# Attention and a gated feed-forward block on one core: score blocks dealt evenly to straight and swapped tiles, another order of the transposes, other weights in the planner

## The chip, the cores and the metric

The kernel runs on one core of a Trainium2 chip. Time is device microseconds of one execution. Before the change the median of three runs is 417.66 us (417.26 to 417.67). The engines are called TensorE (PE in the profile, PEld for its weight loads), VectorE (DVE), ScalarE (ACT), GpSimd (POOL) and SyncE (SP, which issues the DMAs).

## The reference

Causal attention for 4 batches and 12 heads (448 positions, 64 columns a head), then a feed-forward block whose hidden rows are gated by a convolution over three positions. All is float32.

```python
scores = (q @ k.transpose(0, 1, 3, 2)) / np.sqrt(64)
scores = np.where(np.triu(np.ones((S, S), bool), k=1), -1e9, scores)
attn = np.exp(scores - scores.max(-1, keepdims=True))
attn = attn / (attn.sum(-1, keepdims=True) + 1e-9)
x = (attn @ v).transpose(0, 2, 1, 3).reshape(B, S, 768)
h = np.maximum(x @ w_in, 0)                  # 768 -> 1024
c = sum(conv_w[i] * hp[:, i:i + S] for i in range(3))   # hp: h padded by one row
out = (h * (1 / (1 + np.exp(-c)))) @ w_out   # 1024 -> 768
```

## The kernel before

**Attention.** Two heads make a pair, and there are 24 pairs, six for each batch. The rows of the score matrix are cut into seven blocks `k` of 64 queries, and block `k` needs only the keys up to its own end: `KEYS[k] = 64 * (k + 1)`, so 64 to 448 columns. Head `j` lies in partitions `64 * j` on, and each product (L407) uses a quarter of TensorE's array: rows `half(j)` and columns `half(j)`, or the other half for blocks with odd `k`. The first are called straight tiles here, the second swapped tiles. A block takes two products, one for each head. Blocks share four PSUM banks, `SCORES = ((6, 0), (5, 1), (4, 2), (3,))`.

The softmax of a block is a masked minimum of the negated scores (VectorE, L433), an exponential with its sum (ScalarE, L439), an addition and a reciprocal for a group of blocks (VectorE or GpSimd at L455, VectorE at L458), and a scaling by the reciprocal, called normalisation here (VectorE at L470 or ScalarE at L474). Groups are `RANK[:4]` and `RANK[4:]`. Then TensorE transposes the normalised blocks in sixteen 128x128 pieces (L493), four to a PSUM bank. Two banks take turns, and each is copied out (L502, ScalarE or VectorE) before the PV products (L521) use it. `BANKS` says which blocks a bank holds; banks 0 to 3 are filled in this order. Swapped blocks have their heads the wrong way round, and the transpose puts them right.

**Feed-forward.** An operand is split into a rounded upper part and a rest, and three products stand for one: weights upper with activations upper and rest, weights rest with activations upper (L563 for `w_in`, L616 for `w_out`). There are 1152 such products of 448 columns. The 32 weight tiles come as words that need integer steps on VectorE first (L289 or L292, L299 to L315), then a rounding (`round_ways`, L249 to L253: ScalarE, VectorE or GpSimd) and a subtraction for the rest (L263: VectorE or GpSimd). A hidden row block passes through a relu (L574, ScalarE), three taps (L594 on ScalarE or L579 on VectorE, then L581 twice), a tanh (L584), a product (L587), a rounding and a subtraction.

**What sets the order.** Nothing is written out by hand. Each step is added to a `Plan` with its engine, its cost, what it needs and makes, and other ways to do it. `Plan.run` (L64) takes again and again the step that can start first, and among its ways the one whose start plus `cost * WEIGHT` is least (L116). A way marked as holding the port is started only when the port shared by VectorE and GpSimd is free in the plan (L107), and keeps it until its end (L129). The order so found is the program's order on every engine. Pairs of batches 2 and 3 are paced: their scores wait for a count of feed-forward products of the batch before (L410 to L418), and all seven blocks are one step; the others are in two steps of four and three blocks. The planner's numbers that matter are

```python
OWN = {"PE": 0, "DVE": 115, "ACT": 145, "POOL": 40, "SP": 0}
WEIGHT = {"DVE": 1.2, "ACT": 1.0, "POOL": 0.5}
```

## Time and profile before

| what | us |
|---|---|
| median of three runs | 417.66 |
| the profiled execution | 418.87 |
| its span, first to last instruction | 417.1 |
| TensorE busy | 393.9 (94% of the span) |
| VectorE busy | 277.6 (67%) |
| ScalarE busy | 233.5 (56%) |
| GpSimd busy | 115.8 (28%) |

The granted clock of TensorE is 0.98 of full speed over the span. A busy share over the whole span mixes stages: VectorE's 67% is an average of a stage in which it is nearly always busy and of one in which it is busy half the time. A matmul's end is modelled in the trace, so a stretch of TensorE is read from the start of one row to the start of the next. The profile's instructions are two for a float32 product (a record for each of its two passes) and one for a transpose.

### The profile page before, as it was taken

The page shows a single profiled execution, that of the slowest core. Times are in us where ns is not written, and L with a number is a line of the kernel's source. Part 1 is how long each engine was busy: PE and PEld are TensorE (multiplying, and loading weights), DVE is VectorE, ACT ScalarE, POOL GpSimd, SP SyncE. Part 2 cuts the span into 40 slices and gives each one's busy share as a digit, 9 for nine tenths or more (in the row PEclk, how much of TensorE's full clock was granted, in tenths as well). Part 3 has the DMA queues.
Part 4 walks back from the last instruction along what each step waited for, and adds up shares of the span by engine and source line. Part 5 has one row for each costly group of instructions (what it writes and reads, how often), then busy time and mean ns, then how long its engine had stood idle before and what let it go on. Part 6 is the DMA issues. An engine that isn't in the chain of part 4 may idle for free.

```text
span 417.1 us, 7344 instructions
## 1 busy us (share of the span) xinstructions
PE 393.9 (94%) x2604; PEld 305.5 (73%) x2604; DVE 277.6 (67%) x820; ACT 233.5 (56%) x645; POOL 115.8 (28%) x146
## 2 busy tenths in 40 slices
PE   6979977996999999999999999999999999999996
PEld 2646544775766678778778878778778889999895
DVE  3799999999899995548877505548877500477200
ACT  2887886868897755547655616447655611233111
POOL 1032553654565461011231100012231100145300
PEclk9798999998999999999999999999999999999999
DMA  8944502222444743121210222121200011000111
GB/s 282 396 157 152 176 2 77 83 79 68 145 111 138 247 127 107 39 83 46 70 50 22 91 71 67 64 77 46 69 27 3 22 46 44 24 1 0 45 45 44
DMA packets 15156, 35.88 MB, mean 86 GB/s; under 512 B 1808, under 2 KB 4880, under 8 KB 15120
## 3 DMA queue, kind: packets, MB, share of 16 engines
q1 hardware_dynamic: 15120, 35.42, 25.9%
q8 instruction: 20, 0.33, 0.3%
q14 instruction: 16, 0.13, 0.1%
HBM read 29.91 MB, written 5.51 MB: 85 GB/s over the span
## 4 chain that ended last, share of the span: by engine, by line
PE 67%; DVE 23%; ACT 7%; issue 2%; POOL 0%; ACTq 0%; POOLq 0%
PE bank L616 25%; PE bank L563 20%; PE bank L493 8%; PE bank L407 7%; PE bank L521 7%; DVE bank L433 5%; DVE p L470 3%; DVE u L581 2%; DVE wraw L315 2%; DVE u L309 2%; ACT p L439 2%; DVE u L299 2%; ACT pt L502 2%; ACT p L474 1%; DVE u L303 1%
## 5 line engine op out<-in xcount | busy, mean ns | idle before, releaser
L563 PE MATMUL bank<-parts,wih 128*128 128x448 f32 x384 | 116.3, 378 | 3.1 <-DVE parts L537 1.8
L616 PE MATMUL bank<-parts,woh 128*128 128x448 f32 x384 | 114.4, 373 | 0.0
L439 ACT ACTIVATE p<-bank,negm 128x128 f32<-128x128 f32 (+6 forms) x168 | 77.9, 477 | 29.0 <-DVE negm L433 28.1
L563 PEld LDWEIGHTS bank<-parts,wih 128*128 128x128 f32 x384 | 71.8, 191 | 12.2 <-issue 3.6
L433 DVE CUSTOM_DVE_ANT_0 bank<-bank,mask 128x448 f32<-128x448 f32 (+6 forms) x168 | 69.0, 441 | 14.7 <-PE bank L407 12.4
L616 PEld LDWEIGHTS bank<-parts,woh 128*128 128x128 f32 x384 | 71.3, 188 | 8.0 <-issue 2.5
L563 PE MATMUL bank<-parts,wil 128*128 128x448 f32 x192 | 72.8, 379 | 0.0
L493 PE MATMUL bank<-ident,p 128*128 128x128 f32 x384 | 61.3, 288 | 10.5 <-ACT p L474 4.9
L616 PE MATMUL bank<-parts,wol 128*128 128x448 f32 x192 | 71.0, 370 | 0.0
L253 POOL TENSOR_SCALAR parts<-u 128x448 fp32r<-128x448 f32 x27 | 17.2, 638 | 191.4 <-DVE u L587 191.4
L493 PEld LDWEIGHTS bank<-ident,p 128*128 128x128 f32 x384 | 45.8, 145 | 25.0 <-ACT pt L502 9.0
L502 ACT COPY pt<-bank 128x512 f32<-128x512 f32 x89 | 49.9, 585 | 15.8 <-PE bank L493 15.3
L581 DVE SCALAR_TENSOR_TENSOR u<-hr,cw,u 128x448 f32<-128x448 f32 x64 | 50.6, 794 | 6.5 <-ACT u L594 5.1
L407 PE MATMUL bank<-raw 64*64 64x320 f32 (+6 forms) x672 | 51.7, 399 | 3.4 <-ACT p L439 3.2
L521 PE MATMUL bank<-pt,vraw 128*64 128x448 f32 (+3 forms) x384 | 47.3, 387 | 1.4 <-ACT pt L502 1.4
L407 PEld LDWEIGHTS bank<-raw 64*64 64x64 f32 x672 | 27.0, 137 | 26.7 <-issue 11.1
L521 PEld LDWEIGHTS bank<-pt,vraw 128*64 128x64 f32 x384 | 21.5, 137 | 25.7 <-issue 14.8
L563 PEld LDWEIGHTS bank<-parts,wil 128*128 128x128 f32 x192 | 36.7, 191 | 3.8 <-issue 1.1
L263 POOL TENSOR_TENSOR parts<-u,parts 128x448 fp32r<-128x448 f32 x31 | 38.2, 1235 | 2.2
L537 DVE TENSOR_TENSOR parts<-bank,parts 128x448 fp32r<-128x448 f32 x24 | 14.8, 617 | 35.9 <-ACT parts L534 35.6
L616 PEld LDWEIGHTS bank<-parts,wol 128*128 128x128 f32 x192 | 36.1, 188 | 3.4 <-issue 0.8
L627 ACT ACTIVATE u<-bank 128x448 f32<-128x448 f32 x24 | 13.0, 543 | 43.6 <-PE bank L616 42.9
(46 smaller groups left out, 389.9 us busy)
## 6 DMA issues: line engine op xcount, KB each, us to landing
raw<-in_qk_dram SPq DMA_DIRECT2D x24, 448.0 KB, 3.8
vraw<-in_v_dram SPq DMA_DIRECT2D x24, 256.0 KB, 3.0
wraw<-in_w_in_dram SPq DMA_DIRECT2D x16, 384.0 KB, 4.8
wraw<-in_w_out_dram SPq DMA_DIRECT2D x16, 384.0 KB, 3.2
out_dram<-u SPq DMA_DIRECT2D x24, 224.0 KB, 1.9
wraw<-in_conv_w_dram SPq DMA_DIRECT2D x1, 24.0 KB, 6.4
```

The costliest lines, as they stand in the source:

```text
L253: lambda: nc.gpsimd.tensor_scalar(out=out(), in0=src(), scalar1=1.0, scalar2=1.0, op0=ALU.mult, op1=ALU.mult),
L263: engine.tensor_tensor(out=out(), in0=src(), in1=f32(hi()), op=ALU.subtract)
L407: nc.tensor.matmul(at(s)[half(j ^ (k % 2)), o : o + KEYS[k]], lhsT=t[:, 1, 64 * k : 64 * k + 64], rhs=t[:, 0, : KEYS[k]], start=True, stop ...
L433: nc.vector.tensor_tensor_reduce(out=t, in0=t, in1=mask[:, S - n :], scale=-0.125, scalar=3.0e38, op0=ALU.add, op1=ALU.min, accum_out=negm ...
L439: nc.scalar.activation(at(p)[:, :n], at(s)[:, o : o + n], AF.Exp, bias=negm[g % 2][:, c : c + 1], scale=-1.0, accum_out=ssum[g % 2][:, c : ...
L493: nc.tensor.matmul(to, lhsT=at(("p", g, k))[:, P * kc : P * kc + P], rhs=ident, is_transpose=True)
L502: copy(at(part)[:, cols], at(pt))
L521: nc.tensor.matmul(at(pv)[half(j), S - n : S], lhsT=at(vraw)[:, kc, j], rhs=at(("pt", g, y))[:, o : o + 2 * n].rearrange("p (s j q) -> p s ...
L537: nc.vector.tensor_tensor(out=at(x)[:, 1], in0=at(pv)[:, :S], in1=f32(at(x)[:, 0]), op=ALU.subtract)
L563: nc.tensor.matmul(at(ph)[:, :S], lhsT=block(w, NCC * f + cc), rhs=at(x)[:, part], start=q == 0, stop=q == len(prods) - 1)
L581: nc.vector.scalar_tensor_tensor(out=t, in0=src, scalar=w, in1=t, op0=ALU.mult, op1=ALU.add)
L616: nc.tensor.matmul(at(po)[:, :S], lhsT=block(w, NF * m + f), rhs=at(g)[:, part], start=q == 0, stop=q == len(prods) - 1)
```

## The change

There are five edits. Block `k` is on a swapped tile if it is in `SWAPPED = (5, 4, 1, 0)`, and no longer if `k` is odd; the banks of the scores become `((6,), (5, 1), (4, 0), (3, 2))`. The order of the blocks in the scores and in the softmax follows, with groups of three and four blocks in place of four and three. The transpose banks are filled in the order 1, 3, 0, 2: banks 1 and 3 hold nothing but blocks 4 to 6, and the copies' dependences are turned accordingly. In the planner the weight of VectorE goes from 1.2 to 1.5, so that for a step that either engine can do a way on ScalarE is taken more often; and a rounding on GpSimd holds the shared port. The planned cost of the score steps goes from 1850 to 1650 and from 930 to 830.

```diff
-    WEIGHT = {"DVE": 1.2, "ACT": 1.0, "POOL": 0.5}
+    WEIGHT = {"DVE": 1.5, "ACT": 1.0, "POOL": 0.5}
...
-    SCORES = ((6, 0), (5, 1), (4, 2), (3,))
-    RANK = (6, 0, 5, 1, 4, 2, 3)
+    SCORES = ((6,), (5, 1), (4, 0), (3, 2))
+    SWAPPED = (5, 4, 1, 0)
+    RANK = (6, 5, 1, 4, 3, 2, 0)
...
                     out=out(), in0=src(), scalar1=1.0, scalar2=1.0, op0=ALU.mult, op1=ALU.mult
                 ),
+                True,
...
-                        at(s)[half(j ^ (k % 2)), o : o + KEYS[k]], lhsT=t[:, 1, 64 * k : 64 * k + 64],
+                        at(s)[half(j ^ (k in SWAPPED)), o : o + KEYS[k]], lhsT=t[:, 1, 64 * k : 64 * k + 64],
...
-                "PE", 1850, lambda: scores((6, 5, 0, 1, 4, 3, 2)), makes=[("scores", g, 0), ("scores", g, 1)], drop=[raw],
+                "PE", 1650, lambda: scores((6, 5, 1, 3, 4, 2, 0)), makes=[("scores", g, 0), ("scores", g, 1)], drop=[raw],
...
-            for i, blocks in enumerate(((6, 5, 0, 1), (4, 3, 2))):
+            for i, blocks in enumerate(((6, 5, 1), (3, 4, 2, 0))):
...
-        groups = RANK[:4], RANK[4:]
+        groups = RANK[:3], RANK[3:]
...
-        for y, pieces in enumerate(BANKS):
+        TURNS = (1, 3, 0, 2)
+        for z, y in enumerate(TURNS):
+            pieces = BANKS[y]
...
-                        if k % 2:
+                        if k in SWAPPED:
...
-            before_it = ((("pv", g - 1), 1), ("PT", g, 0, 1), ("PT", g, 1, 1), ("PT", g, 2, 1))
             plan.add(
-                "PE", 440, transp, needs=[*names, before_it[y]], mode=3,
+                "PE", 440, transp, needs=[*names, ("PT", g, TURNS[z - 1], 1) if z else (("pv", g - 1), 1)], mode=3,
...
-                needs=[(pt, 1)] + ([("pt", g, y - 1, 0)] if y % 2 else []), makes=[part, ("pt", g, y, 0)],
-                take=[] if y % 2 else [("pt", part)], drop=[pt],
+                needs=[(pt, 1)] + ([("pt", g, y + 1, 0)] if y % 2 == 0 else []), makes=[part, ("pt", g, y, 0)],
+                take=[("pt", part)] if y % 2 else [], drop=[pt],
```

**The scores of the 20th pair on TensorE,** in batch 3, before and after. A row gives the line, the operation, the bank written, the tile read, and the columns of one product; `x2` are the two heads.

```order
L407 MATMUL bank_135<-raw_204 64x448 x2
L407 MATMUL bank_136<-raw_204 64x384 x2
L407 MATMUL bank_135<-raw_204 64x64 x2
L407 MATMUL bank_136<-raw_204 64x128 x2
L407 MATMUL bank_137<-raw_204 64x320 x2
L407 MATMUL bank_138<-raw_204 64x256 x2
L407 MATMUL bank_137<-raw_204 64x192 x2
```

After the change, at the same place:

```order
L409 MATMUL bank_135<-raw_204 64x448 x2
L409 MATMUL bank_137<-raw_204 64x384 x2
L409 MATMUL bank_137<-raw_204 64x128 x2
L409 MATMUL bank_136<-raw_204 64x256 x2
L409 MATMUL bank_138<-raw_204 64x320 x2
L409 MATMUL bank_136<-raw_204 64x192 x2
L409 MATMUL bank_138<-raw_204 64x64 x2
```

Before, the blocks of 448, 64, 320 and 192 columns are on straight tiles (banks 135 and 137) and those of 384, 128 and 256 on swapped ones. After, 448, 256 and 192 are straight (135 and 136) and 384, 128, 320 and 64 swapped (137 and 138).

**The transposes of the same pair on TensorE,** with the feed-forward products between them. Here the names `p_0_215`, `p_0_216` and `p_0_217` are blocks 4, 5 and 6, `p_1_208`, `p_1_210`, `p_1_212` and `p_1_214` blocks 0 to 3; banks 139 and 140 take the transposes; a swapped block is written as `128x2x64`.

```order
L493 MATMUL bank_140<-ident,p_1_208 128x128
L493 MATMUL bank_140<-ident,p_1_210 128x2x64
L493 MATMUL bank_140<-ident,p_1_212 128x128
L493 MATMUL bank_140<-ident,p_1_214 128x2x64
L493 MATMUL bank_139<-ident,p_0_215 128x128
L493 MATMUL bank_139<-ident,p_0_216 128x2x64
L493 MATMUL bank_139<-ident,p_0_217 128x128 x2
L563 MATMUL bank_141<-parts,wih_66 128x448 x2
L493 MATMUL bank_140<-ident,p_1_212 128x128
L493 MATMUL bank_140<-ident,p_1_214 128x2x64
L493 MATMUL bank_140<-ident,p_0_215 128x128
L493 MATMUL bank_140<-ident,p_0_216 128x2x64
```

After the change, from the first transpose of the pair on:

```order
L497 MATMUL bank_140<-ident,p_0_215 128x2x64
L497 MATMUL bank_140<-ident,p_0_216 128x2x64
L497 MATMUL bank_140<-ident,p_0_217 128x128 x2
L497 MATMUL bank_139<-ident,p_0_217 128x128
L497 MATMUL bank_139<-ident,p_0_215 128x2x64
L497 MATMUL bank_139<-ident,p_0_216 128x2x64
L497 MATMUL bank_139<-ident,p_0_217 128x128
L566 MATMUL bank_141<-parts,wil_82 128x448
L566 MATMUL bank_141<-parts,wih_66 128x448
L497 MATMUL bank_140<-ident,p_1_208 128x2x64
L497 MATMUL bank_140<-ident,p_1_210 128x2x64
L497 MATMUL bank_140<-ident,p_1_212 128x128
```

Before, eight transposes that need all of blocks 0 to 6 come first, then four and four. After, eight that need blocks 4 to 6 alone come first, and then the other eight in one piece.

**ScalarE's queue in the softmax of the fifth pair,** in batch 0. `L439` is an exponential, `L474` a normalisation, `L502` a copy of transposes, `L289` and `L249` steps of a weight, `L534` a copy of a PV result.

```order
L439 ACTIVATE p_0_215,ssum_131<-bank_136,negm_129 128x320
L534 CAST parts<-bank_140 128x448
L439 ACTIVATE p_0_211,ssum_131<-bank_136,negm_129 128x192
L439 ACTIVATE p_0_213,ssum_131<-bank_137,negm_129 128x256
L474 ACTIVATE p_0_207<-p_0_207,rcp_133 128x64
L289 ACTIVATE u_220<-wraw 128x384
L289 ACTIVATE u_221<-wraw 128x384
L474 ACTIVATE p_0_213<-p_0_213,rcp_133 128x256
L502 COPY pt_218<-bank_139 128x512
L502 COPY pt_218<-bank_140 128x512
L289 ACTIVATE u_222<-wraw 128x384
L502 COPY pt_219<-bank_139 128x512
```

After the change (lines are two or three higher):

```order
L441 ACTIVATE p_0_207,ssum_131<-bank_137,negm_129 128x64
L537 CAST parts<-bank_139 128x448
L476 ACTIVATE p_0_217<-p_0_217,rcp_133 128x448
L291 ACTIVATE u_222<-wraw 128x384
L476 ACTIVATE p_0_209<-p_0_209,rcp_133 128x128
L476 ACTIVATE p_0_215<-p_0_215,rcp_133 128x320
L476 ACTIVATE p_0_211<-p_0_211,rcp_133 128x192
L291 ACTIVATE u_220<-wraw 128x384
L505 COPY pt_218<-bank_140 128x512
L505 COPY pt_219<-bank_139 128x512
L291 ACTIVATE u_221<-wraw 128x384
L505 COPY pt_218<-bank_140 128x512
```

Four normalisations stand on ScalarE in place of two, larger ones among them, and the copies go to the two halves in turn.

Steps that changed engine, counted in the program up to the first softmax step of the 13th pair (the first of batch 2) on VectorE's and on ScalarE's queue:

| step | VectorE before | after | ScalarE before | after |
|---|---|---|---|---|
| normalisation of 448 columns | 6 | 4 | 6 | 8 |
| of 320 | 6 | 2 | 6 | 10 |
| of 256 | 7 | 1 | 5 | 11 |
| of 192 | 2 | 3 | 10 | 9 |
| of 64 | 4 | 6 | 8 | 6 |
| copy of a transpose bank | 7 | 4 | 41 | 44 |
| copy of a PV result | 0 | 2 | 12 | 10 |
| first tap of the convolution | 2 | 0 | 6 | 8 |
| sign bit cleared, or magnitude | 6 | 4 | 26 | 28 |
| rounding of a weight | 0 | 0 | 2 | 12 |
| rounding of a gate | 0 | 0 | 3 | 4 |
| subtraction for a rest | 5 | 0 | | |
| addition before a reciprocal | 4 | 9 | | |

On GpSimd, over the whole program, roundings of weights go from 30 to 20, their subtractions from 28 to 32, roundings of gates from 27 to 23, subtractions there from 31 to 32. On TensorE 226 of the 1152 feed-forward products stand before the PV products of the 12th pair, and 222 after the change; the scores of the 13th pair come after 241 products, and now after 270.

## Rows read from the trace of the kernel before

**Rows 1.** Busy time of each engine in four stretches of the span (the third lies inside the second). Columns: from and to in us, length, then for PE, PEld, DVE, ACT and POOL the busy us and in brackets the number of instructions, the granted clock of TensorE as a share of full speed, the mean busy share of the DMA engines, GB/s.
```profile
0.00:22.30 22.30, 17.63 (x131) 9.75 (x131) 12.94 (x62) 12.13 (x41) 2.70 (x13) 0.85 0.92 335
22.30:152.90 130.60, 115.87 (x814) 80.71 (x814) 126.56 (x360) 103.18 (x288) 67.13 (x83) 0.97 0.39 121
40.00:61.30 21.30, 18.79 (x160) 11.15 (x152) 21.11 (x70) 18.22 (x54) 11.34 (x14) 1.00 0.30 104
152.90:417.10 264.20, 260.43 (x1663) 215.01 (x1662) 138.06 (x400) 118.15 (x317) 46.00 (x50) 1.00 0.14 48
```

**Rows 2.** The page's chain of work that ended last, as shares of the span by engine, and a piece of the same chain between 40 and 97 us. Columns of the piece: start, us, engine and tile and line, instructions.
```profile
PE 67%; DVE 23%; ACT 7%; issue 2%; POOL 0%; ACTq 0%; POOLq 0%
...
85.16 1.51 DVE u L581
```

**Rows 3.** Timeline of TensorE. First a pair of the fourth batch: its score matmuls and what TensorE started next; then a pair of the second batch of which only blocks 6, 5, 0 and 1 are run in one go. Columns: start us, length us up to the modelled end of the last, engine, line, operation, tiles, shape of the first, count of records. The next row's start shows when the engine was free.
```profile
293.56 1.95 PE L407 MATMUL bank<-raw 64*64 64x448 f32 x28
295.44 0.47 PE L563 MATMUL bank<-parts,wih 128*128 128x448 f32 x1
...
86.35 1.09 PE L407 MATMUL bank<-raw 64*64 64x448 f32 x16
87.37 0.47 PE L563 MATMUL bank<-parts,wil 128*128 128x448 f32 x1
```

**Rows 4.** Timeline of TensorE around the transposes of one pair (from 285.93) and of the next (from 300.61), with the feed-forward products between them. Columns as in rows 3.
```profile
285.93 1.03 PE L493 MATMUL bank<-ident,p 128*128 128x128 f32 x8
286.71 0.64 PE L563 MATMUL bank<-parts,wih 128*128 128x448 f32 x2
287.20 0.66 PE L493 MATMUL bank<-ident,p 128*128 128x128 f32 x4
287.61 0.45 PE L563 MATMUL bank<-parts,wil 128*128 128x448 f32 x1
287.90 0.60 PE L493 MATMUL bank<-ident,p 128*128 128x128 f32 x4
288.25 0.45 PE L563 MATMUL bank<-parts,wih 128*128 128x448 f32 x1
...
300.61 1.39 PE L493 MATMUL bank<-ident,p 128*128 128x128 f32 x8
301.75 0.45 PE L563 MATMUL bank<-parts,wil 128*128 128x448 f32 x1
302.04 0.36 PE L563 MATMUL bank<-parts,wih 128*128 128x448 f32 x1
302.24 0.66 PE L493 MATMUL bank<-ident,p 128*128 128x128 f32 x4
```

**Rows 5.** Groups of VectorE instructions between 22.3 and 152.9 us, shapes kept apart. Columns: line, engine, operation, tiles, output shape and input shape, count, busy us and mean ns of one, idle time before them and what ended it.
```profile
L502 DVE COPY pt<-bank 128x512 f32<-128x512 f32 x6 | 4.1, 684 | 0.2 <-PE bank L493 0.2
...
L470 DVE TENSOR_SCALAR p<-p,rcp 128x320 f32<-128x320 f32 x5 | 2.6, 530 | 0.0
...
L470 DVE TENSOR_SCALAR p<-p,rcp 128x256 f32<-128x256 f32 x6 | 2.3, 389 | 0.0
...
L292 DVE TENSOR_SCALAR u<-wraw 128x384 uint32<-128x384 uint32 x5 | 2.1, 421 | 0.0
L470 DVE TENSOR_SCALAR p<-p,rcp 128x448 f32<-128x448 f32 x4 | 2.1, 515 | 0.0
L263 DVE TENSOR_TENSOR wil<-wraw,wih 128x384 fp32r<-128x384 f32 x3 | 2.0, 670 | 0.0
...
L470 DVE TENSOR_SCALAR p<-p,rcp 128x64 f32<-128x64 f32 x3 | 1.8, 594 | 0.0
...
L579 DVE TENSOR_SCALAR u<-hr,cw 128x448 f32<-128x448 f32 x2 | 1.2, 588 | 0.0
```

**Rows 6.** Groups of ScalarE instructions in the same stretch, columns as in rows 5.
```profile
L502 ACT COPY pt<-bank 128x512 f32<-128x512 f32 x38 | 21.6, 582 | 5.0 <-PE bank L493 4.8
...
L289 ACT ACTIVATE u<-wraw 128x384 f32<-128x384 f32 x25 | 13.9, 566 | 4.2 <-DVE wraw L315 3.7 <-DMA wraw<-in_w_out_dram 0.4
...
L534 ACT CAST parts<-bank 128x448 fp32r<-128x448 f32 x10 | 5.4, 544 | 1.5 <-PE bank L521 1.5
...
L474 ACT ACTIVATE p<-p,rcp 128x448 f32<-128x448 f32 x6 | 4.0, 666 | 3.8 <-DVE rcp L458 3.8
L594 ACT ACTIVATE u<-hr,cw 128x448 f32<-128x448 f32 x6 | 4.0, 663 | 0.2 <-POOL parts L263 0.2
...
L474 ACT ACTIVATE p<-p,rcp 128x320 f32<-128x320 f32 x5 | 2.8, 556 | 1.7 <-DVE rcp L458 1.7
...
L474 ACT ACTIVATE p<-p,rcp 128x256 f32<-128x256 f32 x5 | 2.5, 497 | 0.0
...
L249 ACT CAST wih<-wraw 128x384 fp32r<-128x384 f32 x1 | 0.5, 544 | 0.0
```

**Rows 7.** Two neighbouring VectorE instructions, the GpSimd instruction that ran beside the second, and the group of GpSimd's weight subtractions between 22.3 and 152.9 us. Columns of the first three as in rows 3, of the last as in rows 5.
```profile
67.06 0.35 DVE L303 TENSOR_SCALAR u<-u 128x384 uint32<-128x384 uint32 x1
67.33 0.69 DVE L299 TENSOR_SCALAR u<-u 128x384 f32<-128x384 f32 x1
...
67.25 0.55 POOL L253 TENSOR_SCALAR wih<-wraw 128x384 fp32r<-128x384 f32 x1 [1.47 <-DVE wraw L315]
...
L263 POOL TENSOR_TENSOR wil<-wraw,wih 128x384 fp32r<-128x384 f32 x13 | 13.8, 1064 | 1.1
```

More of the change, by code (lines that the diff above doesn't have):

```diff
@@ L419, in pair @@
         else:
-            for i, blocks in enumerate(((6, 5, 0, 1), (4, 3, 2))):
+            for i, blocks in enumerate(((6, 5, 1), (3, 4, 2, 0))):
                 plan.add(
-                    "PE", 930, lambda blocks=blocks: scores(blocks), makes=[("scores", g, i)], drop=[raw], mode=1,
+                    "PE", 830, lambda blocks=blocks: scores(blocks), makes=[("scores", g, i)], drop=[raw], mode=1,
                     needs=[raw, ("scores", g, 0) if i else ("norm", g - 2)], take=[("S", ("S", g, 2 * i + z)) for z in range(2)],
                 )
-        groups = RANK[:4], RANK[4:]
+        groups = RANK[:3], RANK[3:]
         for i, blocks in enumerate(groups):
@@ L450, in pair @@
         for i, blocks in enumerate(groups):
-            cols = slice(4 * i, 4 * i + len(blocks))
+            cols = slice(3 * i, 3 * i + len(blocks))
             def r_sum(engine, cols=cols):
```

## Prediction

> **What bounds the kernel now.** I read the busy time by stretch first. It splits the span of 417.1 us in three [rows 1]. From 22.3 to 152.9 us VectorE is busy 126.56 of 130.6 us (97%), ScalarE 103.18 (79%), TensorE 115.87 (89%). From 152.9 us on TensorE is busy 260.43 of 264.2 us and VectorE 138.06. So VectorE sets the pace until about 153 us, TensorE after that. The first 22.3 us are start-up, with DMA at a share of 0.92.
>
> The chain of waits says the same [rows 2]: between 40 and 97 us it runs through VectorE, the taps at 85.16 being one of its longer pieces, and over the whole span TensorE's matmuls hold 67%. What the change does is therefore priced twice: in VectorE and ScalarE time before 153 us, and in TensorE time behind it.
>
> **Part 1: the score products.** In the timeline of TensorE a pair's 28 score matmuls (14 products; each float32 product leaves two records) take from 293.56 to the next work at 295.44, so 1.88 us [rows 3]. Where only blocks 6, 5, 0 and 1 are run, 16 matmuls take from 86.35 to 87.37, 1.02 us [rows 3]. Products on straight tiles and on swapped tiles run side by side; the longer of the two streams decides. Before, straight tiles (blocks 6, 4, 2, 0) carry 448+320+192+64 = 1024 columns and swapped ones (5, 3, 1) 768; for blocks 6, 5, 0, 1 it is 512 against 512. So 512 more columns cost 1.88 - 1.02 = 0.86 us, 1.68 ns a column. That the streams overlap follows from the same rows: 1792 columns at 1.68 ns one after the other would take 3.0 us and not 1.88. After the change straight tiles (6, 3, 2) carry 896 and swapped ones (5, 4, 1, 0) 896: 128 columns less on the longer stream, 128 x 1.68 = 0.215 us for each pair. The 12 pairs of batches 2 and 3 stand behind 152.9 us, where TensorE is the bound: 12 x 0.215 = 2.6 us. For the first 12 pairs I count nothing, since there TensorE waits for VectorE. Bounds: 0, if the even deal keeps one stream waiting for the other in some other way, and 24 x 0.215 = 5.2 us.
>
> **Part 2: the order of the transposes.** A pair now has transposes in three places on TensorE: eight from 285.93 to 286.71 (0.78 us), four from 287.20 to 287.61, four from 287.90 to 288.25 [rows 4], 1.54 us together. After, it is two places of eight, 1.56 us. Each return from transposes to products makes the first product about 0.29 us long (287.61 to 287.90) instead of 0.2 (302.04 to 302.24) [rows 4]; one return less saves 0.09 us, 12 pairs 1.1 us. Against it, the second eight need both transpose banks copied out first, and ScalarE takes 0.582 us for a copy [rows 6]. One such wait is seen: the eight at 300.61 take until 301.75, 1.14 us instead of 0.78 [rows 4]. A wait of 0.36 us in every pair would cost 4.3 us. Between -1.1 and +4.3 I take +0.3, because of the pairs I read only this one waited. Early normalisation of blocks 4 to 6 lets the first eight start sooner, but nothing waits there after 153 us.
>
> **Part 3: steps moved between VectorE, ScalarE and GpSimd.** The counts are those in the section on the change, up to the 13th pair, the stretch that VectorE bounds. VectorE loses, by the means of that stretch [rows 5]: 6 normalisations of 256 columns x 0.389, 4 of 320 x 0.530, 2 of 448 x 0.515, 3 transpose copies x 0.684, 2 taps x 0.588, 2 bit-clears x 0.421, and 5 rest subtractions x 0.670 (the row of three of them stands for all): 2.33 + 2.12 + 1.03 + 2.05 + 1.18 + 0.84 + 3.35 = 12.9 us. It gains 2 normalisations of 64 columns x 0.594, 2 casts of a PV result (sized by the copy out of the same kind of bank, 0.684), and 6 small steps (one normalisation of 192 columns and five additions on 3 or 4) that I put at 0.2 each: 3.8 us. Records overlap: an instruction of 0.35 us at 67.06 is followed by the next at 67.33, 0.08 earlier than its end [rows 7]. There are 24 steps less and 10 more, so 14 x 0.08 = 1.1 us comes off: VectorE is relieved of 12.9 - 3.8 - 1.1 = 8.0 us.
>
> ScalarE gains [rows 6]: 6 x 0.497 + 4 x 0.556 + 2 x 0.666 (normalisations), 3 x 0.582 (copies), 11 x 0.544 (roundings of ten weights and a gate), 2 x 0.663 (taps), 2 x 0.566 (magnitudes): 2.98 + 2.22 + 1.33 + 1.75 + 5.98 + 1.33 + 1.13 = 16.7 us. It loses 3 short normalisations (put at 0.4 each) and 2 casts x 0.544, 2.3 us. It has 25 steps more, and with the overlap taken as on VectorE 25 x 0.08 = 2.0 us come off 14.4. So it gains 12.4 us and stands at 103.2 + 12.4 = 115.6 us.
>
> GpSimd does 10 weight roundings less and 4 weight subtractions more. They touch VectorE too: while a rounding ran on GpSimd from 67.25 for 0.55 us, a VectorE step started at 67.33 took 0.69 us instead of the 0.35 of its neighbour [rows 7]. So each rounding gone frees 0 to 0.34 us, 0 to 3.4 us in all; each subtraction that arrives blocks 0 to its own length, 1.064 us [rows 7], 0 to 4.3 us in all. I take half of either: 8.0 + 1.7 - 2.1 = 7.6 us of relief for VectorE. On GpSimd's lock the Trainium skill says more, on its page "SBUF — State Buffer", section "SBUF: two separate sides": VectorE and GpSimd share one pair of ports, and whichever starts first holds it for its whole instruction while the other fully blocks. The row at 67.33 agrees; how often the two meet no page can say, and by it alone the relief could lie anywhere from 3.7 to 11.4 us.
>
> What becomes late next is ScalarE. If VectorE stays the bound with its 4.0 us of idle time, the stretch takes 130.6 - 7.6 = 123.0 us and ScalarE would be busy 94% of it. The highest share that a stretch shows for ScalarE is 18.22 of 21.30 us, 86%, from 40 to 61.3 [rows 1]; at that share 115.6 us of work need 135.1 us, 4.5 more than before. Behind each step added to ScalarE's queue stand the exponentials and the copies of the transposes, for which TensorE waits. VectorE has shown that a queue here can run at 97% once it is the one waited for, and ScalarE's 86% was measured while it was not. So I stand nearer to the first: two thirds of 123.0 and a third of 135.1 is 127.0 us, 3.6 us saved. One thing goes against it: when the 12th pair's PV products are reached, the new order has put 222 products of the feed-forward part before them, the old one 226. The 4 left for later cost 4 x 0.2 = 0.8 us, since TensorE is the bound from there.
>
> **The sum.** 418.87 us of the profiled execution (1.8 us outside the span) - 3.6 + 0.8 - 2.6 + 0.3 = 413.8. The median of the runs is 417.66, 1.2 us under it, so 412.6 us. Behind 153 us VectorE and ScalarE have slack (138.06 and 118.15 busy of 264.2 [rows 1]), so what is moved between them there costs nothing; without this cover each tap moved to ScalarE would make the way to its gate 0.663 - 0.588 = 0.1 us longer.
>
> **Rivals.**
> 1. ScalarE becomes the bound and the stretch to 153 us grows. For it: 12.4 us more on a queue that was never over 86% busy. Against: part of its idle time is waiting for VectorE, which goes as VectorE is relieved. At 86% the stretch costs +4.5; with the rest of the sum (0.8 - 2.6 + 0.3 = -1.5) the whole is 417.66 + 4.5 - 1.5 = 420.7 us. It decides the sign where ScalarE stays below 115.6 / (130.6 + 1.5) = 87.5%.
> 2. The two engines only change places and nothing is gained before 153 us; only TensorE's saving is left: 417.66 - 1.5 = 416.2 us. That is ScalarE at 115.6 / 130.6 = 88.5%.
> 3. VectorE remains the only bound and all relief counts: 417.66 - 7.6 - 1.5 = 408.6 us; with all 10 roundings having been in its way and none of the 4 subtractions, 417.66 - 11.4 - 1.5 = 404.8 us. The rule of the Trainium skill quoted above is a reason one would expect this.
> 4. The even deal doesn't shorten the scores, because one stream is held up by the order in which products are issued: only part 3 acts, 417.66 - 3.6 + 0.8 + 0.3 = 415.2 us. Against it: two streams of uneven length already run side by side in 1.88 us.
>
> **Chances.** Forecast 0.42; rival 1 0.14; rival 2 0.17; rival 3 0.20; rival 4 0.07. No change can be told within 0.2% (0.8 us). All cases but rival 1 lie below 416.8, rival 2 only just; so 0.10 for same (half of rival 2 and a rest of rival 1), 0.13 for slower and 0.77 for faster. The range from 406 to 419.5 leaves out the far end of rival 3 and of rival 1. The forecast's own range is 410 to 415.
>
> **What would show it.** Part 1: a pair's 28 score matmuls take 1.66 to 1.68 us behind 160 us; still 1.88 means rival 4. Part 2: two places of eight transposes; over 0.8 us for the second eight in most pairs means the copies hold them. Part 3: the PV products of the 12th pair start at about 149.3 instead of 152.9 us; VectorE's busy time falls by some 8 us before that point and ScalarE's rises by 12; if ScalarE's share stays at 86% or less and the point moves later, rival 1 holds. From that point to the end 264.2 us should shrink by 1.5.

## The result, and the profile after

The changed kernel takes 403.94 us (median of four runs, 402.56 to 404.97), the kernel before 417.67 beside it: a ratio of 0.966 (95% interval 0.962 to 0.970). The forecast was 412.6 us, with a range down to 406: 13.7 us were gained where 5 were expected. The profiled execution has a span of 400.8 us (before 417.1). These two spans differ by 16.3 us, more than the medians do: the profiled execution before was one of the longer ones of its kernel (418.87), the one after the shortest of its four (402.56).

Busy time by stretch, the view of [rows 1], with the cut at the 12th pair's PV products (135.7 us now, 152.9 before):

```profile
0.00:22.30 22.30, 16.72 (x144) 9.57 (x144) 14.32 (x72) 14.24 (x45) 2.67 (x13) 1.00 0.93 346
22.30:135.70 113.40, 106.58 (x794) 75.98 (x794) 106.03 (x326) 107.63 (x305) 57.45 (x67) 1.00 0.39 125
135.70:400.80 265.10, 260.39 (x1667) 216.77 (x1666) 136.33 (x386) 130.71 (x337) 52.24 (x64) 1.00 0.16 53
```

The first stage is 17.2 us shorter, the rest 0.9 us longer. Up to the cut VectorE is busy 14.32 + 106.03 = 120.4 us, before 12.94 + 126.56 = 139.5; ScalarE 121.9 after 115.3. In the second stretch VectorE (106.03 of 113.4) and ScalarE (107.63, 95%) are now even. The granted clock, 0.97 there before, is 1.00.

The chain of waits of the changed kernel, against [rows 2]:

```profile
PE 62%; DVE 18%; ACT 15%; issue 3%; POOL 1%; DMA 1%; ACTq 0%; DVEq 0%; POOLq 0%
```

VectorE went from 23% to 18% of the span, ScalarE from 7% to 15%: the chain changes between them.

TensorE's timeline in the changed kernel: transposes of one pair and the scores of a later one, columns as in [rows 3] and [rows 4].

```profile
284.23 1.09 PE L497 MATMUL bank<-ident,p 128*128 128x128 f32 x8 [0.50 <-DVE p L472]
285.08 0.66 PE L566 MATMUL bank<-parts,wih 128*128 128x448 f32 x2
285.57 1.13 PE L497 MATMUL bank<-ident,p 128*128 128x128 f32 x8
286.46 0.45 PE L566 MATMUL bank<-parts,wil 128*128 128x448 f32 x1
...
291.76 1.75 PE L409 MATMUL bank<-raw 64*64 64x448 f32 x28
293.43 0.67 PE L566 MATMUL bank<-parts,wih 128*128 128x448 f32 x2
```

Scores take 1.67 us from start to start (293.43 - 291.76) where they took 1.88. The transposes stand in two places: 0.85 us, and 0.89 us with no wait named.

VectorE's four bit steps on the weights, from 22.3 us to the 12th pair's PV products; first the kernel before, then the changed one. Columns as in [rows 5].

```profile
L315 DVE SCALAR_TENSOR_TENSOR wraw<-wraw,u 128x384 uint32<-128x384 uint32 x30 | 18.0, 601 | 0.1
L309 DVE SCALAR_TENSOR_TENSOR u<-wraw,u 128x384 uint32<-128x384 uint32 x29 | 16.9, 583 | 0.1
L303 DVE TENSOR_SCALAR u<-u 128x384 uint32<-128x384 uint32 x30 | 14.4, 480 | 0.1
L299 DVE TENSOR_SCALAR u<-u 128x384 f32<-128x384 f32 x30 | 13.8, 465 | 0.1
```

```profile
L317 DVE SCALAR_TENSOR_TENSOR wraw<-wraw,u 128x384 uint32<-128x384 uint32 x28 | 17.5, 628 | 0.1
L311 DVE SCALAR_TENSOR_TENSOR u<-wraw,u 128x384 uint32<-128x384 uint32 x28 | 15.6, 560 | 0.1
L301 DVE TENSOR_SCALAR u<-u 128x384 f32<-128x384 f32 x27 | 11.4, 425 | 0.1
L305 DVE TENSOR_SCALAR u<-u 128x384 uint32<-128x384 uint32 x27 | 10.6, 396 | 0.0
```

The same work on the same shapes takes 63.1 / 119 = 530 ns a step before and 55.1 / 110 = 501 ns now. Undisturbed such steps take 0.55 and 0.35 us; the rest is time in which GpSimd holds VectorE up. Two or three weight tiles are also converted later than before.

ScalarE's groups in the changed kernel, from 22.3 to 135.7 us, against [rows 6]:

```profile
L505 ACT COPY pt<-bank 128x512 f32<-128x512 f32 x38 | 20.5, 591 | 0.8 <-PE bank L497 0.8
...
L476 ACT ACTIVATE p<-p,rcp 128x448 f32<-128x448 f32 x8 | 5.7, 709 | 0.0
...
L476 ACT ACTIVATE p<-p,rcp 128x320 f32<-128x320 f32 x9 | 5.1, 565 | 1.2 <-DVE rcp L460 1.2
...
L250 ACT CAST wih<-wraw 128x384 fp32r<-128x384 f32 x7 | 3.9, 564 | 0.5 <-DVE wraw L317 0.4
```

The idle time ahead of copies fell from 5.0 to 0.8 us, that ahead of normalisations of 448 columns from 3.8 to 0: ScalarE's idle time was waiting for others, and it went.

**Two measures used below, both to the 12th pair's PV products.** *Blocked*: what VectorE's instructions (from the first pair's PV products on) took beyond their shape's undisturbed length, taken as the 20th percentile over all traces, where that is over 60 ns. *Stall*: the time of the mark less the work that TensorE had issued by then, at 0.203 us a feed-forward product, 0.103 a transpose, 1.883 a pair's PV products, a pair's scores as measured, and 4.0 for the twelve products on zeros at the start. It holds waits and lost clock alike. Before: blocked 17.1 us, stall 40.0. After: 8.7 and 26.1.

**The sum.** At the cut, 17.2 us are the stall's 13.9, 12 x 0.202 = 2.4 of scores, and 0.8 for four products fewer before it. Behind it: scores -2.4, transposes +1.1, those four products +0.8, and the rest mostly new waits before the first transposes of a few pairs (0.50 us at 284.23 above, 0.62 at 191.34): +0.9. Together that is the 16.3 us between the two traces.

### The profile page after: what moved, and what is told of

Its sections match the earlier page's. It is cut to its first block, busy times and chain, and to the rows that moved or that the text cites. A ratio compares the mean times of both kernels' runs of the same rounds, so it can differ in the third digit from the quotient of the medians.

```text
span 400.8 us, 7332 instructions
## 1 busy us (share of the span) xinstructions
PE 383.7 (96%) x2604; PEld 302.3 (75%) x2604; DVE 256.7 (64%) x782; ACT 252.6 (63%) x685; POOL 112.4 (28%) x144
## 4 chain that ended last, share of the span: by engine, by line
PE 62%; DVE 18%; ACT 15%; issue 3%; POOL 1%; DMA 1%; ACTq 0%; DVEq 0%; POOLq 0%
PE bank L619 26%; PE bank L566 18%; PE bank L497 6%; ACT p L441 6%; PE bank L524 6%; DVE bank L435 5%; PE bank L409 4%; ACT pt L505 2%; DVE p L472 2%; DVE u L584 2%; DVE u L311 2%; DVE wraw L317 2%; DVE parts L540 1%; ACT p L476 1%; DVE u L301 1%
## 5 line engine op out<-in xcount | busy, mean ns | idle before, releaser
L566 PE MATMUL bank<-parts,wih 128*128 128x448 f32 x384 | 114.2, 374 | 1.0 <-ACT hr L577 0.4
L619 PE MATMUL bank<-parts,woh 128*128 128x448 f32 x384 | 112.8, 371 | 0.3 <-POOL parts L265 0.3
L441 ACT ACTIVATE p<-bank,negm 128x192 f32<-128x192 f32 (+6 forms) x168 | 78.6, 487 | 27.7 <-DVE negm L435 27.6
L435 DVE CUSTOM_DVE_ANT_0 bank<-bank,mask 128x448 f32<-128x448 f32 (+6 forms) x168 | 68.7, 442 | 15.9 <-PE bank L409 9.7
L497 PE MATMUL bank<-ident,p 128*128 128x128 f32 x384 | 52.5, 280 | 5.3 <-DVE p L472 2.2
L497 PEld LDWEIGHTS bank<-ident,p 128*128 128x128 f32 x384 | 41.5, 141 | 16.8 <-ACT pt L505 5.0
L409 PE MATMUL bank<-raw 64*64 64x256 f32 (+6 forms) x672 | 46.9, 386 | 4.3 <-ACT p L441 4.2
L409 PEld LDWEIGHTS bank<-raw 64*64 64x64 f32 x672 | 28.4, 132 | 25.6 <-issue 13.1
L265 POOL TENSOR_TENSOR parts<-u,parts 128x448 fp32r<-128x448 f32 x32 | 40.7, 1275 | 18.0 <-ACT parts L250 15.9
L254 POOL TENSOR_SCALAR parts<-u 128x448 fp32r<-128x448 f32 x23 | 13.5, 587 | 104.6 <-DVE u L590 103.7
L630 ACT ACTIVATE u<-bank 128x448 f32<-128x448 f32 x24 | 13.2, 549 | 43.7 <-PE bank L619 43.5
L524 PEld LDWEIGHTS bank<-pt,vraw 128*64 128x64 f32 x384 | 21.3, 137 | 25.7 <-issue 13.6
L476 ACT ACTIVATE p<-p,rcp 128x256 f32<-128x256 f32 (+6 forms) x72 | 33.5, 519 | 5.9 <-DVE rcp L460 5.9
```

What stands on the lines that cost most here:

```text
L254: lambda: nc.gpsimd.tensor_scalar(out=out(), in0=src(), scalar1=1.0, scalar2=1.0, op0=ALU.mult, op1=ALU.mult),
L265: engine.tensor_tensor(out=out(), in0=src(), in1=f32(hi()), op=ALU.subtract)
L409: nc.tensor.matmul(at(s)[half(j ^ (k in SWAPPED)), o : o + KEYS[k]], lhsT=t[:, 1, 64 * k : 64 * k + 64], rhs=t[:, 0, : KEYS[k]], start=Tru ...
L435: nc.vector.tensor_tensor_reduce(out=t, in0=t, in1=mask[:, S - n :], scale=-0.125, scalar=3.0e38, op0=ALU.add, op1=ALU.min, accum_out=negm ...
L441: nc.scalar.activation(at(p)[:, :n], at(s)[:, o : o + n], AF.Exp, bias=negm[g % 2][:, c : c + 1], scale=-1.0, accum_out=ssum[g % 2][:, c : ...
L476: nc.scalar.mul(t, t, rcp[g % 2][:, c : c + 1])
```

## The experiments

Ratios are to the kernel before, timed beside each. Its own median lay between 417.7 and 419.4 us there, so differences of a microsecond or two between medians of different rows are not sure. "Planner" means the weight 1.5 and the port held by GpSimd's roundings; "deal" the new `SCORES`, `SWAPPED`, groups, block order and planned cost of the score steps; "turns" the new order of the transpose banks.

| kernel | us | ratio, 95% interval | blocked | stall |
|---|---|---|---|---|
| before | 417.7 | 1 | 17.1 | 40.0 |
| planner alone (e1) | 415.58 | 0.993 (0.991 to 0.996) | 15.0 | 35.8 |
| deal and turns alone (e2) | 418.07 | 0.999 (0.997 to 1.001) | 18.2 | 40.1 |
| all but the port (e3) | 418.72 | 1.001 (0.999 to 1.003) | 22.1 | 41.3 |
| all but the weight (e4) | 410.25 | 0.981 (0.978 to 0.984) | 6.8 | 32.4 |
| planner and deal (e6) | 409.35 | 0.978 (0.975 to 0.980) | 9.0 | 31.8 |
| planner and turns (e10) | 411.16 | 0.982 (0.980 to 0.984) | 8.0 | 28.5 |
| after | 403.94 | 0.966 (0.962 to 0.970) | 8.7 | 26.1 |

**The two halves of the change.** Planner alone, and deal and turns alone:

```diff
-    WEIGHT = {"DVE": 1.2, "ACT": 1.0, "POOL": 0.5}
+    WEIGHT = {"DVE": 1.5, "ACT": 1.0, "POOL": 0.5}
...
+                True,
```

> The kernel before with the planner's two edits alone (VectorE's weight 1.5, a rounding on GpSimd holds the port); deal, softmax order and transpose order as before. Theory A (the 17 us won before the 12th pair's PV products come from VectorE being relieved, by steps moved off it and by GpSimd's roundings out of its way): most of the gain is here, 405 to 409 us; the 5 us missing at most are the scores' 24 x 0.2 us. Theory B (they come from the new block and transpose order, by which the first eight transposes need not wait for the whole softmax): 413 to 418 us. VectorE's mean for the two integer steps at L299 and L303 should fall from 0.45 and 0.47 to about 0.40 by A.

> The changed kernel with the planner's numbers of before (weight 1.2, a rounding on GpSimd doesn't hold the port): only the deal and the two orders are new. A: 412 to 416 us (2.4 us from the scores of the last 12 pairs, little before). B: 404 to 407 us. VectorE's normalisations before the 13th pair are 31 in this program against 25 in the changed one and 34 before.

The planner alone gives 2.4 us (415.58, in theory B's range), deal and turns alone nothing (418.07, outside both ranges). The sum of the two is far from 13.7: on top of the planner's edits, deal and turns are worth 415.58 - 403.94 = 11.6 us.

**The planner's two edits one at a time,** each taken out of the changed kernel: the port (the line `True,`), and the weight (back to 1.2).

> The changed kernel without the port flag on GpSimd's roundings. Its program has 54 roundings on GpSimd (43 in the changed one, 57 before) and 34 normalisations on VectorE up to the 13th pair (25 in the changed one). A with GpSimd's share of it (the port flag matters): 409 to 414 us, L299 and L303 at 0.45 again. If the weight is what counts: 404 to 406 us.

> The changed kernel with VectorE's weight back at 1.2 and the port flag kept. Its program has 35 roundings on GpSimd and 26 normalisations on VectorE. If the port flag is what counts, 404 to 407 us; if the weight is, 409 to 414 us.

Without the port nothing is left of the gain (418.72, above both expected ranges) and VectorE is blocked for 22.1 us. With the port and the old weight it is 410.25, in the range that made the weight count. With deal and turns in place the port alone is worth 418.07 - 410.25 = 7.8 us, and the weight on top of it 6.3; the weight without the port is worth nothing (418.72 against 418.07). What the missing port does is seen in VectorE's timeline of that kernel, and under it in GpSimd's, columns as in [rows 7]:

```profile
72.12 0.34 DVE L304 TENSOR_SCALAR u<-u 128x384 uint32<-128x384 uint32 x1
72.39 0.69 DVE L300 TENSOR_SCALAR u<-u 128x384 f32<-128x384 f32 x1
73.00 1.39 DVE L310 SCALAR_TENSOR_TENSOR u<-wraw,u 128x384 uint32<-128x384 uint32 x1
```

```profile
72.29 0.58 POOL L254 TENSOR_SCALAR wih<-wraw 128x384 fp32r<-128x384 f32 x1 [1.79 <-DVE wraw L316]
72.95 1.03 POOL L264 TENSOR_TENSOR wil<-wraw,wih 128x384 fp32r<-128x384 f32 x1
```

A rounding started at 72.29 and its subtraction at 72.95. The step at 72.39 takes 0.69 us in place of 0.35, the one at 73.00 1.39 in place of 0.55; it ends 0.41 us after the subtraction does (74.39 against 73.98), less than its own undisturbed length. In the changed kernel a subtraction on GpSimd, and VectorE beside it, the minimum of the softmax (L435), which works in a PSUM bank:

```profile
84.89 1.37 POOL L265 TENSOR_TENSOR wol<-wraw,woh 128x384 fp32r<-128x384 f32 x1 [4.27 <-ACT woh L250]
```

```profile
84.69 0.68 DVE L584 SCALAR_TENSOR_TENSOR u<-hr,cw,u 128x448 f32<-128x448 f32 x1
85.29 0.17 DVE L460 RECIPROCAL rcp<-rcp 128x4 f32<-128x4 f32 x1
85.37 0.47 DVE L435 CUSTOM_DVE_ANT_0 bank<-bank,mask 128x320 f32<-128x320 f32 x1
```

Here VectorE loses nothing: 0.47 us, where L435 takes 0.51 on average at this size. Over the whole trace before, 55 such minima beside a subtraction took 443 ns on average, and others of the same sizes 450; bit steps with one operand took 887 ns where one ran beside most of the step (eight of them) and about 395 otherwise. Copies out of a bank, over the traces with subtractions, took 684 ns beside one and 687 beside nothing. A subtraction is harmless beside work in a bank. Of the subtractions' time up to the cut, 46% lay beside VectorE's work in banks before, 36% without the port (e3), 50% in the changed kernel and 63% in e4.

**Is it the luck of one order?** The planner's cost of a switch from 100 to 105 shakes the order and means nothing else.

```diff
-    SWITCH = 100
+    SWITCH = 105
```

> The changed kernel with one number of the planner nudged that has nothing to do with the change (the planned cost of a change between kinds of TensorE work, 100 to 105): the same edits, another of the orders that the planner can find (15 more products are behind the 12th pair's PV products). If the gain belongs to the edits: 401 to 406 us. If much of it is the luck of one order: 407 to 413 us.

> The kernel before with the same nudge, 100 to 105. If the order before was an ordinary one: 415 to 420 us. If it was an unlucky one: 408 to 414 us; then part of the 13.7 us is not the change's.

> The kernel before with the planner edits alone (weight 1.5, port held by GpSimd's roundings), and the planner's cost of a switch 105 in place of 100, which only shakes the order. Without the shake it was 415.58 us; the kernel before with the same shake alone was 423.71 us. If the planner edits have a steady worth, they take the same 2 us off again or more: 418 to 421 us, VectorE's time beside GpSimd below the 19.2 us of the shaken kernel before. If an order's luck is as large as that worth: anywhere from 410 to 424 us.

> The changed kernel without its planner edits (weight 1.2, no port held by roundings), shaken in the same way (105 in place of 100). Without the shake it was 418.07 us; the whole changed kernel with the shake was 405.76 us. Theory of the interaction (the deal and the order pay only where VectorE is kept clear of GpSimd): 415 to 421 us, VectorE's time beside GpSimd 15 us or more. Rival F (the one order was lucky): a time nearer to 410 us, or above 423.

Shaken: before 423.71, planner 414.31, deal and turns 418.06, all 405.76 us. So one order's luck is worth 0 to 2 us here, and 5 to 6 in the kernel before, which got slower than either range expected: its own order was not an unlucky one. The planner alone came out below the range for a steady worth, in that of luck. With the means of each pair (420.7, 414.9, 418.1, 404.9) the halves are worth 5.8 and 2.6 and the whole 15.8: 7.4 us appear only together. The interaction is larger than the scatter of three of the four pairs; against the fourth it is not by much. Blocked times are 19.2, 13.6 and 13.9 us, and 9.6 for all. The 13.9 of deal and turns is less than the 15 expected, and hardly more than the planner's 13.6, though that kernel is 3.8 us slower: blocked time alone does not set the time.

**Deal and turns.** Old turns in the changed kernel, with the copies' dependences turned back too; then the old deal, in a version that leaves block 0 in block 6's bank but in the second group, and in a clean one (before, with planner and turns).

```diff
-        TURNS = (1, 3, 0, 2)
+        TURNS = (0, 1, 2, 3)
```

> The changed kernel with the transpose banks filled in the old order 0, 1, 2, 3, all else new. Theory D (the order of the transposes matters little: the prediction's part 2 is +0.3 us, measured +1.07 us behind the 12th pair): 402.5 to 404.5 us. Theory E (the early transposes of blocks 4 to 6 let the copies start earlier, and this is what relieves the pairs in front): 408 us or more, with longer TensorE waits for copies and normalisations in the first 12 pairs. Rival F (luck of the order): anything from 402 to 412 us, without a change of the waits for the copies.

```diff
-    SCORES = ((6,), (5, 1), (4, 0), (3, 2))
-    SWAPPED = (5, 4, 1, 0)
+    SCORES = ((6, 0), (5, 1), (4, 2), (3,))
+    SWAPPED = (5, 3, 1)
```

> The changed kernel with the old deal alone: banks ((6, 0), (5, 1), (4, 2), (3,)), odd blocks on swapped tiles; the order of the transposes, the order of the steps and the planner's numbers are the new ones. Theory D (the deal's worth is TensorE work alone, 24 x 0.202 = 4.9 us where TensorE is never waited out): 403.9 + 4.9 = 408.8 us, scores of a pair at 1.88 us, TensorE's time beside its work as in the changed kernel (38 us). Theory E (the bank that block 6 has for itself is what ends the long waits of the first pairs, before and up to pair 3 5.4 us of TensorE's stalls): 403.9 + 4.9 + about 5 = 414 us, a granted clock under 1 near 10 us, TensorE's stalls at 43 us or more. Rival F (what was gained is one lucky order; any edit of this size loses it): 412 to 420 us with stalls spread over the whole span.

> The kernel before with the planner edits and the new order of the transposes, but the old deal with its old banks and groups of four and three (in the earlier run without the new deal block 0 shared the bank of block 6 while it was in the second group, which holds that bank longer; here it is in the first). Reached step by step the change is then: planner -2.1, the deal with its banks -6.2 (409.35 against 415.58), the order of the transposes -5.4. Theory of single worths: 415.58 - 5.4 = 410.2 us, within 2. Theory of an interaction (the new order of the transposes pays only where blocks 6 and 5 and 1 are a group of their own, so that blocks 4 to 6 are ready early): 414 us or more, with the first eight transposes waiting for normalisations.

The old turns give 409.35 us, in theory E's range. The first version of the old deal was badly made: 421.24 us (1.005, 1.003 to 1.008), with a stall of 31.9 us at the cut that grows to 50.5 at the end, where the changed kernel goes from 26.1 to 38.0; most likely because the bank of blocks 6 and 0 is then held by both groups. It does not price the deal. The clean one gives 411.16, as single worths would have it. Planner alone 415.58, with turns 411.16, with the deal 409.35, with both 403.94: the turns are worth 4.4 or 5.4 us, the deal 6.2 or 7.2, whichever comes first. These two nearly add up (10.6 us of the 11.6, by the smaller of each), though each stands on one order, which can move a time by the microseconds just seen; the theory that the turns need the new groups fell. Without the planner edits both together are worth nothing (e2).

How much of the deal is the evenness of the streams? 960 columns on the longer one, banks, groups and order kept:

```diff
-    SWAPPED = (5, 4, 1, 0)
+    SWAPPED = (5, 3, 2, 1)
```

> The changed kernel with blocks 5, 3, 2 and 1 on swapped tiles in place of 5, 4, 1 and 0: 960 columns on the longer stream in place of 896 (before the change 1024), while banks, groups and every order stay. Theory D (the longer stream alone decides): 64 x 1.68 = 0.107 us more for a pair's scores, so 1.785 us, and for 12 to 24 pairs 1.3 to 2.6 us, a time of 405.2 to 406.5 us. Rival G (the new banks and groups are what matters, the evenness of the streams nothing): 403.9 us within 1.

404.78 us, 0.967 (0.965 to 0.969): 0.8 us more by the medians, which is in rival G's range and which the intervals don't separate from nothing. A pair's scores take 1.78 us, as theory D has it. Its trace by stretch:

```profile
22.30:135.60 113.30, 106.76 (x796) 75.93 (x796) 105.79 (x326) 107.49 (x305) 57.54 (x67) 1.00 0.39 126
135.60:402.60 267.00, 261.87 (x1667) 216.07 (x1666) 138.78 (x386) 130.84 (x336) 50.62 (x64) 1.00 0.16 52
```

The 12th pair's PV products stand at 135.6 us, where they were at 135.7: a score shorter or longer by 0.1 us is worth nothing before that point. Behind it 265.1 became 267.0 us; 12 x 0.107 = 1.3 of this was expected. So of the deal's 6.2 to 7.2 us the even streams are some 2.4 (12 pairs, 128 columns, 0.202 us each); that the other part comes from banks, groups and the order of blocks follows by exclusion alone.

**Which engine limits the first stage?** A copy nobody needs, in each of the first 12 pairs, on ScalarE, or on VectorE with `nc.vector.tensor_copy(scratch[:, :383], mask[:, :383])` behind the minimum:

```diff
+    scratch = sb.tile([P, S], F32, name="scratch")
...
+                    if b < 2 and c == NB - 1:
+                        nc.scalar.copy(scratch, mask)
```

> The kernel before, order unchanged, with one more ScalarE instruction in each of the first 12 pairs (a copy of 448 columns to an unused tile, about 0.47 us, 5.6 us in all). If VectorE alone bounds the first 150 us (my prediction's reading of before): 0 to 2 us longer. If ScalarE is as much on the path: 3 to 6 us longer.

> The kernel before, order unchanged, with one more VectorE instruction in each of the first 12 pairs (383 columns, an odd count and one SBUF input, about 0.47 us, 5.6 us in all). VectorE bounds: 4 to 7 us longer. Otherwise 0 to 3.

> The changed kernel with the same extra ScalarE instruction. ScalarE is 92 to 100% busy from 20 to 120 us in its trace. Theory C (ScalarE has become the bound, so a microsecond on it costs one, and it was not held at 86%): 3 to 6 us longer. If VectorE is still the only bound: 0 to 2.

> The changed kernel with the same extra VectorE instruction. By C (ScalarE bound, VectorE nearly): 1 to 4 us longer, less than in the kernel before. If VectorE is still the only bound: 4 to 7.

The copies on VectorE, by group, in the kernel before and in the changed one:

```profile
L439 DVE CAST scratch<-mask 128x383 f32<-128x383 bf16 x12 | 5.8, 480 | 0.0
```

```profile
L441 DVE CAST scratch<-mask 128x383 f32<-128x383 bf16 x12 | 8.3, 688 | 0.0
```

Ratios: before 1.0045 (ScalarE) and 1.0064 (VectorE), after 0.9688 and 0.976 where it was 0.9662. That is 1.9 and 2.7 us before, 1.1 and 4.1 after, for copies that took 6.9 and 5.8 us before, 7.5 and 8.3 after. So no engine alone sets the pace in either kernel, at least not at the place of the copy, behind a pair's last block: each costs well under its own time. After, VectorE is still the dearer one by far, part of it because eight of its twelve copies met a subtraction on GpSimd (688 ns on average, 355 undisturbed); ScalarE at 95% is not the new bound.

**GpSimd's subtractions replaced by fills,** in the kernel before (n1) and in the changed one (n2).

```diff
+            if engine is nc.gpsimd:
+                for _ in range(2):
+                    engine.memset(f32(out()), 0.0)
+                return
```

> The kernel before in its own order, but each subtraction on GpSimd (59 of them) is replaced by two fills of the same tile, which read nothing: the rest part of those operands is left out (zero). Engines and order stay. Up to the 12th pair's PV products VectorE spends 17.1 us more on its instructions than the undisturbed ones of the same form need, 16 of it beside GpSimd's work. Theory A1 (VectorE blocked by GpSimd's reads is on the path to the end): the excess falls to 1 to 3 us and the time by 10 to 15 us, to 403 to 408 us. Theory B1 (VectorE's blocked time is in the shadow of other waits): the excess falls too, the time by under 4 us, 414 us or more.

> The same replacement in the changed kernel (64 subtractions), whose excess is 8.7 us. A1: the time falls by 5 to 8 us, to 396 to 399 us, and what is left of the difference to the kernel before without subtractions is 6 to 9 us of the 13.7: 4.9 of it TensorE's work for the scores and the rest steps moved to ScalarE. B1: 401 us or more.

414.44 us (0.989, 0.986 to 0.991) before, 402.44 (0.959, 0.956 to 0.963) after. Both lie in the ranges of theory B1, that blocked time is in the shadow of other waits. But the test was weak: fills hold VectorE up as well, and its blocked time only fell from 17.1 to 13.2 and from 8.7 to 5.5 us. In n1's trace the 12th pair's PV products come 3.9 us earlier (149.0 against 152.9), with the granted clock at half for 6.8 us up to there in place of 13.7. In n2's they come 0.4 us later (136.1 against 135.7), and the intervals of its ratio and of the changed kernel's touch. What a microsecond of blocked time is worth is not shown by this.

## Why the prediction was wrong

**Two steps of the sum failed. The first is the netting of GpSimd's port in part 3.** It gave each rounding that goes 0 to 0.34 us and each subtraction that comes 0 to 1.064, took half of either, and netted them to 0.4 us against VectorE. Measured, the blocked time fell by 8.4 us. By the GpSimd work beside it: with a rounding among it from 7.0 to 1.8 us, with subtractions alone or beside an addition from 10.1 to 6.9, though there were 35 of them in place of 33. Three things were wrong. The count was only that of the weights (10); up to the cut 13 roundings are gone. The bound of 0.34 us came from one row. And the sign of the subtractions was taken from their number, where what matters is what VectorE does beside each. (VectorE's whole time up to the cut fell by 19.1 us: 8.4 of it blocked time, 10.7 work, where 8.0 had been worked out; ten bit steps fewer, of conversions that stand later, are in it.)

Put -8.4 in place of +0.4 and VectorE's relief is 8.0 + 8.4 = 16.4 us; the stage became 17.2 shorter. That this sum nearly closes is in part luck. The 17.2 us belong to two traces that differ by more than the medians; the copies priced VectorE's time at about half of itself; and e4, with 6.8 us blocked, is 6.3 us slower than the changed kernel with 8.7. What is shown is that without the port's hold nothing is left of the gain (e3); the prediction never worked out what the planner does with it.

**The second is the "nothing" that parts 1 and 2 counted for the deal and the turns before the cut.** The reason given, that TensorE waits there for VectorE, does not hold alone: the extra copy on VectorE cost 2.7 us in the kernel before, of 5.8. On top of the planner's edits deal and turns are worth 11.6 us, where -2.6 + 0.3 stood in the sum; the stall up to the cut falls by 4.2 us with the planner alone (40.0 to 35.8) and by 9.7 more with them. They act on the port's term too. With the planner alone blocked time with a rounding among it is down to 1.4 us, but that with subtractions is up to 13.6; with the deal added it is 7.6 (e6), with the turns 7.0 (e10). A sum of single worths could not see this.

**ScalarE's ceiling of 86% was wrong.** It runs at 95% in the second stretch. Rival 1 and the third of the weight given to 135.1 us rested on it. Its added time was also overstated: 6.6 us up to the cut in place of 12.4. The steps were counted nearly right (21 more up to the cut, 25 counted); what was mis-sized is their overlap. The lengths of ScalarE's records add up to 17.4 us more than before, but neighbours now overlap by 40.9 us in place of 30.1, since in a queue that seldom waits nearly every step starts before its predecessor's record ends. The prediction took 2.0 us off for this.

**The clock was not looked at.** [Rows 1] show 0.97 in the second stretch and the prediction passes over it. Busy time and clock of the kernel before, in three short stretches:

```profile
10.00:15.00 5.00, 4.64 (x33) 2.95 (x34) 3.66 (x18) 3.45 (x17) 0.23 (x1) 0.50 1.04 406
...
35.00:40.00 5.00, 5.00 (x35) 3.26 (x37) 4.67 (x21) 4.38 (x16) 1.57 (x3) 0.81 0.35 92
100.00:105.00 5.00, 4.76 (x21) 4.13 (x22) 3.69 (x7) 5.00 (x13) 2.69 (x3) 0.68 0.29 80
```

The granted clock is at the lower of its two levels (1.2 and 2.4 GHz) for all or part of each. The timeline of the kernel before shows what TensorE did ahead of each:

```profile
5.14 2.45 PE L407 MATMUL bank<-raw 64*64 64x448 f32 x28
10.36 3.79 PE L407 MATMUL bank<-raw 64*64 64x448 f32 x28 [2.77 <-ACT p L439]
14.09 3.30 PE L493 MATMUL bank<-ident,p 128*128 128x128 f32 x16
...
30.19 0.33 PE L493 MATMUL bank<-ident,p 128*128 128x128 f32 x1 [0.36 <-DVE p L470]
...
31.47 0.33 PE L493 MATMUL bank<-ident,p 128*128 128x128 f32 x1 [0.95 <-DVE p L470]
...
32.55 1.09 PE L493 MATMUL bank<-ident,p 128*128 128x128 f32 x6 [0.76 <-ACT p L474]
...
96.56 1.13 POOL L263 TENSOR_TENSOR parts<-u,parts 128x448 fp32r<-128x448 f32 x1
96.62 1.49 DVE L315 SCALAR_TENSOR_TENSOR wraw<-wraw,u 128x384 uint32<-128x384 uint32 x1
98.14 0.53 ACT L249 CAST woh<-wraw 128x384 fp32r<-128x384 f32 x1 [1.36 <-DVE wraw L315]
...
99.64 1.16 PE L493 MATMUL bank<-ident,p 128*128 128x128 f32 x6 [3.07 <-ACT p L474]
```

In the first it stood idle for 2.77 us, and the second pair's scores then took 14.09 - 10.36 = 3.7 us in place of 1.88. Ahead of the second it waited three times for normalisations. The third is a chain that starts at the port: the bit step at 96.62 took 1.49 us in place of 0.55 beside GpSimd's subtraction; a rounding on ScalarE waited 1.36 us for it; a normalisation was queued behind that rounding and a tap; TensorE waited 3.07 us for the normalisation. The same place in the first 18 us of the changed kernel:

```profile
4.99 1.75 PE L409 MATMUL bank<-raw 64*64 64x448 f32 x28
7.64 0.97 PE L409 MATMUL bank<-raw 64*64 64x448 f32 x4 [0.90 <-ACT p L441]
8.91 1.08 PE L409 MATMUL bank<-raw 64*64 64x384 f32 x8 [0.30 <-ACT p L441]
10.57 0.97 PE L409 MATMUL bank<-raw 64*64 64x256 f32 x16 [0.59 <-ACT p L441]
```

Block 6 has a bank to itself, so the second pair's scores start at 7.64, as soon as that one is read, and go on in pieces; no wait in these rows is over 0.90 us, and the clock stays at 1.00. The lower level covers 13.7 us in all before, so it cost at most 6.9 us of the 13.9 of stalls. It was likely less: of 61 executions of the kernel before that stand beside the experiments, the 24 with a mean clock of 0.990 or more took 417.6 us on average and the 21 with 0.984 or less 419.1. There 0.8% of clock, some 3.4 us, was worth 1.5 us; at that rate 6.9 is worth an estimated 3. It isn't the cause by itself: deal and turns alone run at a mean of 0.999 and have a stall of 40.1 us, as before. In these three places it follows waits, and makes them dearer.

**What was right.** Part 1: 0.202 us a pair against 0.215 worked out, and the streams that run side by side; 2.4 us behind the cut against 2.6. That nothing is to be had from shorter scores before it is borne out by e9. Part 2: between its bounds, +1.1 us in the transposes of twelve pairs and some 1.2 of new waits ahead of them, in place of +0.3; the second eight take 0.89, over the 0.8 given as the sign that the copies hold them, though the trace names no wait there. The turns' real worth, 4.4 to 5.4 us, lies in the first stage. The part behind the cut grew by 0.9 us where 1.5 less was forecast: the moved products (+0.8) were foreseen, the new waits for a normalisation were costed at nothing. Rival 3 came nearest. Its far end of 404.8 was right that the port frees VectorE of more than the forecast had, and wrong that VectorE be the sole bound, since the copies show both engines in the chain; and it has nothing from deal and turns before the cut. That it lies within 0.9 us of the measured time is luck.

The port's rule in the Trainium skill ("SBUF — State Buffer", section "SBUF: two separate sides") names its lock for VectorE's steps in a two-port mode, or with two inputs in SBUF against a GpSimd step that reads SBUF. The minima in a bank, 443 ns beside a subtraction and 450 without, agree. The 3.7 to 11.4 us of relief that the prediction set beside it lie under the 19.1 measured: what was wrong is how often the two meet, not the rule.

**What stays open.** Why deal and turns pay only where the port is in the plan was not tried by itself. One reading is that an unplanned hold makes the plan's times wrong for what follows; no run separates this from another order as such, and a shaken order alone moves the kernel before by 5 to 6 us. The port without the weight was not tried in the kernel before, and no run separates its two effects, fewer roundings on GpSimd and other times for what stays there. The deal's remaining 4 us were not split between banks, groups and order.

## What to carry to other kernels

Where a planner orders the work, price an edit of its rules by what it does to collisions: list what runs beside what, and separate VectorE's steps in SBUF, which GpSimd's instructions hold up, from its steps in a bank, which they don't. An engine's highest busy share while it waits for another is no ceiling. Test edits of a planner together as well as one at a time: here two halves worth 2.4 us and nothing made 13.7. Shake such a kernel once (a cost changed by 5 ns) before an edit's single worth is believed.

## What was not expected of the hardware

A fill on GpSimd holds VectorE up too, though not every step: in n1 the bit steps with one operand took 571 ns beside a fill alone (five of them) and 334 without, while the convolution's steps with two operands took 685 (six) and 683. A VectorE step that is under way holds GpSimd up in turn: the subtraction at 84.89 took 1.37 us where 15 of the 32 of this shape took 1.01 to 1.04.
